# Two stretches of unused bytes in SBUF that move the operands of the expert and the dense matmuls

## The chip, the core and the metric

The kernel runs on one core of a Trainium2 chip. The metric is the device time of one execution in microseconds, as the median of several runs. Three runs of the kernel before gave 948.05 us (947.99 to 948.15).

## The reference

Attention with a threshold, a routed expert layer that picks one of eight experts for each token, and a dense layer, one behind the other, for 4 x 576 = 2304 tokens of 512 features:

```python
def _attn_ref(q, k, v, tau):          # 4 batches, 8 heads, 576 rows, 64 features
    scores = scale * np.matmul(q, k.transpose(0, 1, 3, 2))
    thresh = np.max(scores, axis=-1, keepdims=True) - tau
    scores = np.where(scores >= thresh, scores, -1000000000.0)
    attn = softmax(scores)
    return np.matmul(attn, v)

def _moe_ref(x, modality_id, w_gate, modality_bias, w1, w2):
    logits = x @ w_gate + modality_bias[modality_id]
    e_idx = np.argmax(logits, axis=1)  # gate_w: the softmax value of the chosen expert
    for e in range(8):
        mask = e_idx == e
        h = np.maximum(x[mask] @ w1[e], 0.0)              # 512 -> 1024
        out[mask] = gate_w[mask, None] * (h @ w2[e])      # 1024 -> 512

def _moe2_ref(x, w_in, w_out):
    h = x @ w_in                                          # 512 -> 2048
    g = h * (1.0 / (1.0 + np.exp(-1.702 * h)))
    return g @ w_out                                      # 2048 -> 512
```

(`softmax(scores)` stands for the reference's lines that subtract the maximum, take the exponential and divide by the sum.)

## The kernel before

The kernel has three stages. The order of the work on each engine is written out by hand, and tiles come from pools that a stack of contexts lays out in SBUF one behind the other.

*Attention* (up to some 310 us) works pair by pair of heads; the change leaves its tiles where they are.

*Experts* (some 310 to 536 us). Tokens are gathered by expert into five slots: four of 512 rows and one of 264. A slot has eight steps f, and each step two groups of 12 matmuls. `Ffn.s1` (L974) multiplies the 128 columns f of the first weights, as the operand that is loaded into the array, with the slot's tokens x, as the operand that is streamed past them: each operand is split into a high and a low part in fp32r (`xh` and `xl`, `ah` and `al`), and the 12 matmuls are four pieces of 128 features times the three products high-high, high-low and low-high. ScalarE and VectorE turn the result into `hh` and `hl`. `Ffn.s2_cols` (L1018) takes the second weights `bh` and `bl` as the loaded operand and `hh` and `hl` as the streamed one, again 12 matmuls, two steps later (`LAG = 2`). The weights come from DRAM into `ra` and `rb` (L1228, L1234) and are split by L1241 and L1242.

*Dense* (some 526 to 935 us). Two blocks of 512 tokens, then two of 512 and one of 256, each with 16 steps f. L974 works as before, with `wi_h` and `wi_l` as the loaded operand and x as the streamed one. `Ffn.s2` (L999) is the other way round: `hh` and `hl` are loaded, 128 tokens at a time, and `wo_h` and `wo_l` are streamed, with 512 columns: four tiles of tokens times three products, 12 matmuls (six in the block of 256). While the first block runs, `convert` splits the last of these weights out of `cv_raw` through `cv_a` into high and low parts (L1143 to L1147, L1152, L1153).

The pools that the change concerns are opened in `moe_kernel` at L1188 to L1193: x, h, sg and ids, then `e_raw` (`ra`, `rb`), `e_w` (`ah` to `bl`) and `e_y` of the experts, then `r_work_b`, the small tiles of the router's second pass. Above them, from the other end of SBUF, lie the resident weights and the tiles of `convert`. When the experts are done, the dense weights that had no room (`wi2`, `wo2`) take the place of the `e_` pools. In the trace they carry the names of `wi_h`, `wi_l`, `wo_h` and `wo_l` like the resident ones.

The built program says where each tile starts in a partition. The remainders of these addresses by 256 bytes:

| tiles | kernel before | changed kernel |
|---|---|---|
| `xh`, `xl` | 64 | 224 |
| `hh`, `hl`, `sg` | 64 | 224 |
| `ra`, `rb`, `ah`, `al`, `bh`, `bl`, `y` | 0 | 224 |
| resident dense weights `wi`, `wo`, and `cv_raw`, `cv_a`, `cv_e` | 224 | 224 |
| later dense weights `wi2`, `wo2` | 224 | 224 |
| `ident`; the four `xg` | 128; 64, 128, 192, 0 | the same |

Inside these tiles a matmul's operands start at multiples of 256 bytes from the tile's start (128 columns of 4 bytes are 512 bytes), so that the table holds for each of them.

Of the kernel before, what the change touches and what calls it, by code (L numbers as in the profile page):

```python
# [8 lines left out]
F32 = mybir.dt.float32  # L9
# [514 lines left out]
PG = 512  # L524
NA = 2
NB = 12
SLOT_ROWS = (512, 512, 512, 512, 264)
SLOT_TILES = tuple(-(-r // 128) for r in SLOT_ROWS)
NB_STATIC = len(SLOT_TILES) - NA
# [3 lines left out]
class Router:  # L533
# [19 lines left out]
    def setup_items(self, tmp_pool):  # L553
# [25 lines left out]
        self.pages = T([128, NE], "pages")  # L579
        self.place = T([128, NB * PG // 128], "place")  # L580
        pl = W([128, NB * PG // 128], "pl", I32)
        flat = midf.rearrange("p b c -> p (b c)")
# [14 lines left out]
        def ids():  # L597
# [4 lines left out]
            nc.gpsimd.tensor_copy(pf, pi)  # L602
            nc.gpsimd.iota(pl, pattern=[[128, NB * PG // 128]], base=1, channel_multiplier=1)
            nc.gpsimd.tensor_copy(self.place, pl)
# [97 lines left out]
    def assign(self, ph, gate):  # L702
        nc, wk = self.nc, self.wk[ph]
        first = ph == "A"
        n = NCOL - 5 if first else NCOL
        ns = NA if first else NB
        nh = ns * PG // 128
        t = {}
        T = lambda shape, name, dt=F32: wk.tile(shape, dt, name=name)
        be = lambda a: a.unsqueeze(1).broadcast_to([128, n, NE])  # L710
        rs, cnt = T([128, n, NE], "rs"), T([128, NE], "cnt")
        f, excl, end, base = (T([128, NE], x) for x in ("f", "excl", "end", "base"))
        ok = T([128, n, NE], "ok")
        plf = T([128, 2, n], "plf")
        OL = T([128, n, 128], "OL", BF16)
        R = T([128, n, 2, nh], "R", BF16)
# [53 lines left out]
        def slots():  # L770
            cmp = T([128, ns, NE], "cmp")
            nc.vector.tensor_tensor(
                cmp, end.unsqueeze(1).broadcast_to([128, ns, NE]),
                self.iota[:, 0:ns].unsqueeze(2).broadcast_to([128, ns, NE]), op=ALU.is_le,
            )
            yield
            t["cmp"] = cmp
            ef = T([128, ns], "ef")
            nc.vector.tensor_reduce(out=ef, in_=cmp, axis=AX.X, op=ALU.add)
            yield  # L780
            ei = self.c.tile([128, ns], I32, name="ei" + ph)
            nc.vector.tensor_scalar(ei, ef, float(NE - 1), None, op0=ALU.min)
            yield
            self.idx["e" + ph] = ei

        sh = T([128, ns], "sh")

        def gaps():

# [9 lines left out]
        def bounds():  # L799

            s0, last = NB_STATIC - 1, SLOT_ROWS[-1]
            total, c = T([128, 1], "total"), T([128, 2], "cc")
            nc.vector.tensor_reduce(out=total, in_=cnt, axis=AX.X, op=ALU.add)
            yield
            nc.vector.tensor_sub(c, self.place[:, 4 * s0:4 * s0 + 8:4], sh[:, s0:s0 + 2])
            yield
            nc.vector.tensor_sub(c, c, self.place[:, 0:1].broadcast_to([128, 2]))
            yield
            nc.vector.tensor_tensor(c, c, total.broadcast_to([128, 2]), op=ALU.min)
            yield  # L810
            over = T([128, 2], "over")
            nc.vector.tensor_sub(over[:, 0:1], c[:, 1:2], c[:, 0:1])
            yield
            nc.vector.tensor_scalar(over[:, 0:1], over[:, 0:1], float(last), None, op0=ALU.is_gt)
            yield
            nc.vector.tensor_scalar(over[:, 1:2], c[:, 1:2], float(REST), None, op0=ALU.is_gt)
            yield
            nc.vector.tensor_tensor(over[:, 0:1], over[:, 0:1], over[:, 1:2], op=ALU.max)
            yield
            nc.vector.tensor_scalar(self.range[:, 0:1], over[:, 0:1], -1.0, float(NB_STATIC), op0=ALU.mult, op1=ALU.add)  # L820
            yield
# [73 lines left out]
        def compact():  # L895
            cp = T([128, nh], "cp")
            nc.vector.tensor_sub(
                cp.rearrange("p (s t) -> p s t", t=4), self.place.rearrange("p (s t) -> p s t", t=4),
                sh.unsqueeze(2).broadcast_to([128, ns, 4]))
            yield  # L900
            nc.vector.scalar_tensor_tensor(out=cp, in0=t["s"], scalar=0.0, in1=cp, op0=ALU.is_ge, op1=ALU.mult)
            yield
            icc = self.c.tile([128, nh], I32, name="iccB")
            nc.vector.tensor_scalar(icc, cp, -1.0, None, op0=ALU.add)
            yield
            c0 = T([128, NB_STATIC], "c0")
            nc.vector.tensor_sub(c0, self.place[:, 0:4 * NB_STATIC:4], sh[:, 0:NB_STATIC])
            yield
            ico = self.c.tile([128, NB_STATIC], I32, name="icoB")
            nc.vector.tensor_scalar(ico, c0, -1.0, None, op0=ALU.add)  # L910
            yield
            self.idx["cB"], self.idx["oB"] = icc, ico

        rest = [] if first else [None]
        return [
            None, ranks, pages, starts, limits, slots, inside, counted, places, digits, *rest, high,
            lambda: (low(0, 5), values(0)), *rest, lambda: (low(5, 10), values(1)), *rest, lambda: low(10, n), gate,
            *[None] * (1 if first else NBW), lambda: sum_up(0, n), lists,
            *([] if first else [None] * 12 + [gaps, compact, None, bounds]),
        ]  # L920

# [117 lines left out]
def moe_kernel(ctx, tc, kq, v, tau, mid, w_gate, mod_bias, w1, w2, w_in, w_out, out):  # L1039
    nc = tc.nc  # L1040
    ctx.enter_context(tc.manual_schedule())
    P = lambda name, bufs, c=ctx, **kw: c.enter_context(tc.tile_pool(name=name, bufs=bufs, **kw))
# [142 lines left out]
                self.step()  # L1185


    x_p, h_p, sg_p, id_p = P("x", 2), P("h", 3), P("sg", 1), P("ids", 2)  # L1188
    ffn.hp = h_p
    ectx, fctx = ExitStack(), ExitStack()  # L1190
    EP = lambda name, bufs: P(name, bufs, c=ectx, reuse_waits="tile")
# [78 lines left out]
    def make_slot(s):  # L1270
# [10 lines left out]
        def rest(d, w):  # L1281
# [4 lines left out]

            n = min(128, SLOT_ROWS[s] - d * 128)
            if n > 0:
# [10 lines left out]
            first if s < NA else rest)  # L1299
        return ffn.xprep(blk, x_p, rows[s], wide=(s == 0), count=SLOT_ROWS[s])  # L1300

# [150 lines left out]
    lo = nc.values_load(router.range[0:1, 0:1], min_val=NB_STATIC - 1, max_val=NB_STATIC)  # L1452
    hi = nc.values_load(router.range[0:1, 1:2], min_val=NB_STATIC, max_val=NB)
    with tc.For_i(lo, hi, 1) as i:
# [107 lines left out]
```

## Time and profile before

| | us |
|---|---|
| median of 3 runs | 948.05 |
| the profiled execution | 946.41 |
| its span, first to last instruction | 944.6 |
| TensorE busy in the span | 910.1 |
| weight loads of TensorE busy | 734.9 |
| VectorE busy | 516.2 |
| ScalarE busy | 455.0 |
| GpSimd busy | 224.8 |

The profile tells an operation by its line, its engine, and the tiles that it writes and reads ("tr<-xh,wi_h": the matmul that writes `tr` from `xh` and `wi_h`). Matmuls are pipelined: the profiled duration of one ends after the start of the next, so that durations of neighbours overlap, and the time between two starts is shorter than a duration. PE is TensorE, PEld its loading of weights, DVE VectorE, ACT ScalarE, POOL GpSimd, SP the engine that issues most of the DMAs. A query can narrow the trace to a stretch, counted in us from the span's start.

### The profile page before, as it was taken

Reading aid. Unit: us, or ns where it says so; the run is one execution under the profiler, and the core shown is the slowest. Engines: PE = TensorE matmul, PEld = TensorE weight load, DVE = VectorE, ACT = ScalarE, POOL = GpSimd, SP = SyncE. Lnnn points to the kernel's source line nnn. Section 1 sums busy time; section 2 is a strip of 40 time slices with the busy share of each in tenths; the row PEclk is TensorE's granted clock in tenths of the full one; section 3 lists DMA queues with packets and bytes.
Section 4 is the critical chain, followed back from the end, with each engine's and each line's share of the span. In section 5 each row is a group of like instructions: output and inputs, shape, how many; then the busy total and the mean of one; then the engine's idle time right before and its main releaser. Section 6 shows DMA issues by size and latency. Waiting matters only on the chain.

```text
span 944.6 us, 13971 instructions
## 1 busy us (share of the span) xinstructions
PE 910.1 (96%) x5015; PEld 734.9 (78%) x5015; DVE 516.2 (55%) x1129; ACT 455.0 (48%) x820; POOL 224.8 (24%) x299
## 2 busy tenths in 40 slices
PE   8899999999987999999999999999999999999995
PEld 7777777777765678878889888888888888888894
DVE  6888888888797375578787587611111111111111
ACT  6777777777766443455545455422222222222231
POOL 4946475566414302010520000010001000100100
PEclk9999999999999999999999999999999999999998
DMA  7655864654504444565746254210001000100100
GB/s 229 152 143 145 227 174 116 165 150 121 133 13 114 141 136 135 180 229 174 237 171 230 71 179 132 91 45 12 23 12 45 6 12 6 45 0 1 45 1 25
DMA packets 64523, 100.72 MB, mean 107 GB/s; under 512 B 10596, under 2 KB 35970, under 8 KB 64450
## 3 DMA queue, kind: packets, MB, share of 16 engines
q1 hardware_dynamic: 61138, 89.84, 32.6%
q0 software_dynamic: 3312, 9.94, 3.3%
q8 instruction: 42, 0.69, 0.3%
q14 instruction: 31, 0.25, 0.1%
HBM read 63.97 MB, written 17.11 MB: 86 GB/s over the span
## 4 chain that ended last, share of the span: by engine, by line
PE 77%; DVE 9%; issue 6%; ACT 3%; DMA 2%; POOL 1%; SPq 1%; POOLq 0%; ACTq 0%; DVEq 0%
PE tr L974 27%; PE sc L999 19%; PE sc L239 9%; PE sc L1018 8%; PE av L353 5%; PE tr L307 5%; DVE e L250 3%; DVE E L280 2%; PE tr L383 1%; PE av L349 1%; ACT e L256 1%; PE tr L328 1%; DVE bl L1242 1%; DMA cv_raw<-in_moe_w_in_dram 1%; PE av L946 1%
## 5 line engine op out<-in xcount | busy, mean ns | idle before, releaser
L1209 DVE TENSOR_TENSOR hl<-sg,hh 128x512 fp32r<-128x512 f32 (+1 forms) x80 | 51.1, 639 | 271.2 <-ACT hh L1207 271.2
L1206 ACT ACTIVATE sg<-tr 128x512 f32<-128x512 f32 (+1 forms) x80 | 44.5, 556 | 238.9 <-PE tr L974 238.8
L250 DVE TENSOR_SCALAR_CACHE_REDUCE e<-sc,taue 128x576 f32<-128x576 f32 x144 | 116.6, 813 | 30.2 <-PE sc L239 25.5
L256 ACT ACTIVATE e<-e,thr 128x576 f32<-128x576 f32 x144 | 111.3, 776 | 27.1 <-DVE e L250 26.5
L239 PE MATMUL sc<-kA,qT 128*128 128x288 f32 x320 | 102.1, 336 | 14.9 <-DVE E L280 11.0
L999 PE MATMUL sc<-wo_h,hh 128*128 128x512 f32 x288 | 114.1, 396 | 0.0
L999 PE MATMUL sc<-wo_h,hl 128*128 128x512 f32 x288 | 113.9, 396 | 0.0
L999 PE MATMUL sc<-wo_l,hh 128*128 128x512 f32 x288 | 113.8, 395 | 0.0
L280 DVE SCALAR_TENSOR_TENSOR E<-sc,thr,e 128x576 f32<-128x576 f32 x128 | 103.7, 815 | 8.4 <-ACT e L256 4.6
L309 ACT COPY AT<-tr 128x512 f32<-128x512 f32 x128 | 74.0, 578 | 39.4 <-PE tr L307 38.6
L239 PE MATMUL sc<-kB,qT 128*128 128x288 f32 x320 | 89.4, 295 | 0.9 <-DVE kB L220 0.9
L239 PEld LDWEIGHTS sc<-kA,qT 128*128 128x128 f32 x320 | 60.2, 188 | 31.7 <-issue 19.4
L974 PE MATMUL tr<-xh,wi_h 128*128 128x512 f32 (+1 forms) x320 | 80.8, 375 | 0.0
L974 PE MATMUL tr<-xl,wi_h 128*128 128x512 f32 (+1 forms) x320 | 80.3, 372 | 0.0
L974 PE MATMUL tr<-xh,wi_l 128*128 128x512 f32 (+1 forms) x320 | 80.1, 372 | 0.0
L307 PE MATMUL tr<-ident,E 128*128 128x128 f32 x512 | 76.7, 272 | 0.0
L353 PE MATMUL av<-AT,V 128*64 128x288 f32 x512 | 76.7, 419 | 0.0
L974 PEld LDWEIGHTS tr<-xh,wi_h 128*128 128x128 f32 x320 | 57.8, 188 | 13.0
L974 PEld LDWEIGHTS tr<-xl,wi_h 128*128 128x128 f32 x320 | 56.9, 188 | 11.9
L974 PEld LDWEIGHTS tr<-xh,wi_l 128*128 128x128 f32 x320 | 56.8, 188 | 11.6
L999 PEld LDWEIGHTS sc<-wo_h,hl 128*128 128x128 f32 x288 | 54.2, 188 | 13.2
L999 PEld LDWEIGHTS sc<-wo_l,hh 128*128 128x128 f32 x288 | 54.3, 188 | 12.3
(219 smaller groups left out, 1569.3 us busy)
## 6 DMA issues: line engine op xcount, KB each, us to landing
ra<-in_moe_w_dram SPq DMA_DIRECT2D x20, 512.0 KB
rb<-in_moe_w_dram SPq DMA_DIRECT2D x20, 512.0 KB
F<-in_kq_dram SPq DMA_DIRECT2D x15, 640.0 KB
cv_raw<-in_moe_w_in_dram SPq DMA_DIRECT2D x16, 512.0 KB
cv_raw<-in_moe_w_out_dram SPq DMA_DIRECT2D x16, 512.0 KB
V<-in_vp_dram SPq DMA_DIRECT2D x16, 320.0 KB
kA<-kA SPq DMA_DIRECT2D x15, 320.0 KB
kB<-kB SPq DMA_DIRECT2D x15, 320.0 KB
```

The lines of the kernel that those rows point to most:

```text
L239: nc.tensor.matmul(sc[:, hf, 0:288], l, d[kk][:, c0 + hf * 288:c0 + (hf + 1) * 288], start=(i == 0), stop=(i == len(ops) - 1),)
L250: nc.vector.tensor_scalar(e, d["sc", w][:, :, 0:288], self.taue[:, 0:1], 3.0e38, op0=ALU.add, op1=ALU.min, accum_out=thr)
L256: self.nc.scalar.activation(d["e", w], d["e", w], ACTF.Exp, bias=d["thr", w][:, 0:1], scale=-1.0)
L280: nc.vector.scalar_tensor_tensor(out=E.rearrange("p (a c) -> p a c", a=2), in0=d["sc", w][:, :, 0:288], scalar=d["thr", w][:, 0:1], in1=d[ ...
L307: nc.tensor.transpose(tp[:, kc * 128:(kc + 1) * 128], E[:, k0 + kc * 128:k0 + (kc + 1) * 128], self.ident)
L309: copies.append(lambda: nc.scalar.copy(AT[:, h, :, c * 128:(c + 1) * 128], tp.rearrange("p (k c) -> p k c", k=4)))
L353: nc.tensor.matmul(d["av"][h * 64:(h + 1) * 64, 0:288], d["V"][:, h, kc, :], d["AT"][:, h, kc, hf * 288:(hf + 1) * 288], start=False, stop ...
L974: nc.tensor.matmul(hps[:, 0:T], w[:, kd, :], blk[x][:, kd, 0:T], start=(i == 0), stop=(i == 11))
L999: nc.tensor.matmul(y, h[:, cs], w, start=(f == 0 and i == 0), stop=(f == blk["nf"] - 1 and i == 2))
L1018: nc.tensor.matmul(blk["y"][d], w[:, ds], h[:, 0:T], start=(f == 0 and i == 0), stop=(f == last and i == 2))
L1206: nc.scalar.activation(sg, hps, ACTF.Gelu_apprx_sigmoid)
L1209: return [upper, lambda: nc.vector.tensor_sub(hl, sg, hh.bitcast(F32))]
```

## The change

A pool with one unused tile of 160 bytes is opened ahead of x, and one with an unused tile of 64 bytes behind ids. To make room for them, the router's second pass shares some of its small tiles: `ef` becomes `sh`, and `c0` and `cc` become one tile `three`. The start of the region above, 147424, stays where it is; the small tiles now end at that address.

```diff
+PHASE = (160, 64)
...
+        sh = T([128, ns], "sh")
+        three = T([128, NB_STATIC], "three")
...
-            ef = T([128, ns], "ef")
+            ef = sh
...
-        sh = T([128, ns], "sh")
-
...
-            total, c = T([128, 1], "total"), T([128, 2], "cc")
+            total, c = T([128, 1], "total"), three[:, 0:2]
...
-            c0 = T([128, NB_STATIC], "c0")
+            c0 = three
...
+    P("phase_x", 1).tile([128, PHASE[0] // 4], F32, name="phase_x")
     x_p, h_p, sg_p, id_p = P("x", 2), P("h", 3), P("sg", 1), P("ids", 2)
+    P("phase_w", 1).tile([128, PHASE[1] // 4], F32, name="phase_w")
```

Built, both programs have the same instructions in the same order on every engine. Their semaphores differ in one place: in `bounds` the first subtraction (L805) now waits for the sum ahead of it (L803), both on VectorE.

## Rows read from the trace of the kernel before

**Rows 1.** Page, part 1: busy us, share of the span, instructions.

```profile
PE 910.1 (96%) x5015; PEld 734.9 (78%) x5015; DVE 516.2 (55%) x1129; ACT 455.0 (48%) x820; POOL 224.8 (24%) x299
```

**Rows 2.** Page, part 4: chain that ended last, shares by engine.

```profile
PE 77%; DVE 9%; issue 6%; ACT 3%; DMA 2%; POOL 1%; SPq 1%; POOLq 0%; ACTq 0%; DVEq 0%
```

**Rows 3.** Stretches: length; PE, PEld, DVE, ACT, POOL busy (instructions); PEclk, DMA share, GB/s.

```profile
410.00:450.00 40.00, 40.00 (x184) 32.91 (x183) 31.82 (x56) 22.98 (x35) 3.57 (x4) 1.00 0.67 226
600.00:650.00 50.00, 50.00 (x216) 40.22 (x215) 13.72 (x22) 14.68 (x26) 3.94 (x4) 1.00 0.15 50
```

**Rows 4.** Waits of the whole span: us in total, times, longest us.

```profile
ACT sg L1206 <- PE tr L974: 238.8, 71, 4.4
```

**Rows 5.** The chain in order of time: start us, us, what.

```profile
411.05 2.75 PE sc L1018 x12
413.80 2.75 PE tr L974 x12
...
511.25 1.45 PE tr L974 x12
...
545.47 2.81 PE tr L974 x12
...
876.28 2.80 PE tr L974 x12
```

**Rows 6.** Groups by form, 300 to 944 us: busy us, mean ns | idle before.

```profile
L999 PE MATMUL sc<-wo_h,hh 128*128 128x512 f32 x288 | 114.1, 396 | 0.0
...
L999 PE MATMUL sc<-wo_l,hh 128*128 128x512 f32 x288 | 113.8, 395 | 0.0
L974 PE MATMUL tr<-xh,wi_h 128*128 128x512 f32 x256 | 70.4, 397 | 0.0
L974 PE MATMUL tr<-xl,wi_h 128*128 128x512 f32 x256 | 70.2, 396 | 0.0
L974 PE MATMUL tr<-xh,wi_l 128*128 128x512 f32 x256 | 69.9, 394 | 0.0
```

**Rows 7.** Two seam matmuls by line: ns min/median/max, first and last start us.

```profile
L974 PE MATMUL tr<-xh,wi_l x1: 392/392/392, 536.7 to 536.7; 128*128 128x512 f32 x1
...
L999 PE MATMUL sc<-wo_h,hl x1: 394/394/394, 926.9 to 926.9; 128*128 128x512 f32 x1
```

**Rows 8.** By line, L974 (600 to 870 us), L1018 (410 to 495 us); columns alike.

```profile
L974 PE MATMUL tr<-xh,wi_h x192: 392/396/403, 601.4 to 865.6; 128*128 128x512 f32 x192
...
L1018 PE MATMUL sc<-hh,bh x60: 388/392/394, 410.9 to 491.3; 128*128 128x512 f32 x60
```

**Rows 9.** Last block: order of time (start us, us), then L974 by line.

```profile
895.85 0.66 PE L974 MATMUL tr<-xh,wi_h 128*128 128x256 f32 x4
...
897.29 0.40 PE L999 MATMUL sc<-wo_h,hh 128*128 128x512 f32 x1
...
L974 PE MATMUL tr<-xh,wi_l x64: 278/282/286, 882.7 to 928.4; 128*128 128x256 f32 x64
```

**Rows 10.** By line, L1018 ahead of a transpose, the first and the last.

```profile
L1018 PE MATMUL sc<-hh,bl x1: 393/393/393, 342.0 to 342.0; 128*128 128x512 f32 x1
...
L1018 PE MATMUL sc<-hh,bl x1: 394/394/394, 493.2 to 493.2; 128*128 128x512 f32 x1
```

**Rows 11.** Groups by form, ScalarE and VectorE, 545 to 944 us.

```profile
L1207 ACT CAST hh<-sg 128x512 fp32r<-128x512 f32 x60 | 37.3, 621 | 1.9
...
L1152 ACT CAST wo_h<-cv_a 128x512 fp32r<-128x512 f32 x10 | 6.2, 620 | 19.0 <-DVE cv_a L1147 19.0
...
L1209 DVE TENSOR_TENSOR hl<-sg,hh 128x512 fp32r<-128x512 f32 x61 | 42.2, 692 | 227.5 <-ACT hh L1207 227.5
...
L1153 DVE TENSOR_TENSOR wo_l<-cv_a,wo_h 128x512 fp32r<-128x512 f32 x10 | 6.9, 692 | 6.5 <-ACT wo_h L1152 6.4
```

**Rows 12.** Stretches with a load of ra, then of cv_raw; columns as in rows 3.

```profile
378.80:382.00 3.20, 3.20 (x16) 2.62 (x15) 0.23 (x1) 0.86 (x2) 0.00 (x0) 1.00 0.97 355
559.20:562.00 2.80, 2.80 (x14) 2.25 (x13) 2.65 (x6) 1.95 (x4) 0.00 (x0) 1.00 0.91 322
```

## The prediction

> **What bounds the kernel now.** I read the page's first line: TensorE is busy for 910.1 of 944.6 us [rows 1]. Then the shares of the chain of work that ended last: 77% of the span lies on TensorE [rows 2]. Then stretches of the dense stage: from 600 to 850 us each of five times 50 us has TensorE busy for all 50.00 us, 216 matmuls, at the full granted clock (1.00 of 2.4 GHz), while VectorE and ScalarE are busy for 8 to 15 us; the first of the five stands there [rows 3]. It is the others that wait: ScalarE for L974, 238.8 us in all [rows 4]. So from some 537 us on, time is the number of matmuls times the **pitch**, the time from the start of one to the start of the next, and only a change of pitch moves the end.
>
> The pitch is not one number. In the chain a group of 12 matmuls of 512 columns takes 2.80 or 2.81 us in the dense stage and 2.75 us in the expert stage [rows 5], where TensorE is as full, 40.00 of 40 us [rows 3]. From 545.47 to 876.28 us lie 59 rounds of 24 matmuls: 330.81 / 1416 = 233.6 ns. In the expert stage it is 2.75 / 12 = 229.2 ns. Clock and columns are the same. What differs is where the operands lie. While matmul k streams its moving operand, the weights of matmul k+1 are loaded beside it, so the moving operand of k and the weights of k+1 are the pair that can get in each other's way. By the table of remainders this pair is 64 and 0 in the expert stage, 64 and 224 for L974 in the dense stage, 224 and 64 for L999. I call a step **equal** if both remainders are the same. The dense stage has such steps already, at its seams: from the last L974 of a group to the first L999 (64 and 64), and from the last L999 to the first L974 (224 and 224).
>
> The trace tells the seams from the rest by the profiled durations. A duration runs on past the next start by a nearly fixed time: dense 395.9 against 233.6 ns of pitch, expert 392 against 229.2, so 162 to 163 ns in both. Differences of duration are therefore differences of pitch. The 62 seams from L974 to L999 last 390 to 393 ns, the 77 from L999 to L974 392 to 394 ns; the first of the one kind and the last of the other stand in [rows 7]. Inside the groups the durations spread, for L974 from 392 to 403 ns [rows 8].
>
> **The change part by part.** The 160 bytes ahead of the x tiles take x, h and sg from 64 to 224; with the 64 bytes behind the ids the expert weights go from 0 to 224; the dense weights stay at 224. All steps inside the tiles are multiples of 256 bytes, so every L974, L999 and L1018 step becomes equal. No instruction is added, removed or moved on any engine, and the DMA issues stay in their order.
>
> *Dense, 512 columns.* L974 has 768 of these, 256 each with means of 397, 396 and 394 ns; L999 has 864, of which two thirds show 396 and one third 395 [rows 6]. Take the seams out, 64 at 391.5 ns (62 of them before L999) and 77 at 393: the other 704 of L974 last (768 x 395.7 - 64 x 391.5) / 704 = 396.0, the other 786 of L999 395.9. I use 395.9 for both. What will an equal step cost when it follows an equal step? No long chain of them is in the trace. From below it is bounded by the shortest durations of the expert stage, 388 ns [rows 8]; from above by an equal step of another kind, L1018 followed by a transpose whose f32 weights also lie at 64: there are 16 of these, the first at 393, the last at 394 ns [rows 10], with a mean of 394.3 and a spread of 390 to 399. I take the mean of the two kinds of seams, 392.2: they have the lines, types and widths of the steps in question, and they came out within 4 ns of each other although the steps ahead of them did not. Gain: 1490 x (395.9 - 392.2) = 5.5 us.
>
> *Dense, 256 columns.* 192 of L974 in the last block, 12 of them in 897.29 - 895.85 = 1.44 us [rows 9]. The seam among the 12 lasts 278 ns, the shortest that this pair of tiles shows there [rows 9], so its pitch is 278 - 163 = 115; the other 11 take (1440 - 115) / 11 = 120.5. Gain: 176 x 5.5 = 1.0 us.
>
> *Expert, 512 columns.* 768 matmuls at a median of 392 ns [rows 8]. They give up the good pair of 64 and 0: by pitch 392.2 - 162.4 = 229.8 against 229.2, so 0.6 x 768 = 0.5 us is lost, between nothing and 0.9 us.
>
> *Expert, 264 columns.* 192 of them, 12 in 1.45 us [rows 5], a pitch of 120.8. The seam's 115 at 256 columns would be 118.6 at 264 ones, 0.4 us gained; no equal step of this width is in the trace, so between nothing and 0.4, and I take 0.2.
>
> *VectorE and ScalarE at the new places.* The same operations stand in the trace at 64 and at 224: ScalarE's copies 621 (L1207) and 620 ns (L1152), VectorE's subtractions 692 (L1209) and 692 ns (L1153) [rows 11]. I cost them at nothing; most of each stretch is free for them [rows 3]. The router's shared small tiles put one more wait between two VectorE operations that follow each other anyway, in the stretch from 410 to 450 us, where TensorE is busy without a break [rows 3]: nothing.
>
> *The weight loads.* The expert weights now land at 224 instead of 0. A stretch with a load of ra at 0 moved 355 GB/s at a busy share of 0.97, one with a load of cv_raw, which is at 224 already, 322 at 0.91 [rows 12]: 366 and 354 for a full share. The 3% between them on 1.5 us for 512 KB is 0.05 us for each of 40 loads, issued groups ahead of their use: costed at nothing, 2 us if all of it were uncovered. The Trainium skill (DMA: Bandwidth & Descriptors, How a descriptor splits into AXI transactions) says that a descriptor which does not start at a multiple of 256 bytes pays for a first transaction from the boundary below; by that, a piece of 1 KB at 224 costs 39 beats in place of 32, and 20 loads of ra, uncovered, some 6 us, an estimate from that page that would eat the gain. The trace's 354 against 366 shows a far smaller difference.
>
> **Sum.** 5.5 + 1.0 - 0.5 + 0.2 = 6.2 us. Nothing is late in its place: what feeds TensorE in the dense stage waits for it [rows 4]. The profiled execution took 946.41 us, 1.8 of it outside the span, and would take 940.2; the median of the runs, 948.05, becomes 941.9.
>
> **Rivals.** *Deeper:* a chain of equal steps settles at the 388 ns that the expert stage shows in part of its steps. Dense 7.9 x 1490 = 11.8, expert 4 x 768 = 3.1, the narrow ones 1.2: 16.1 us, 932.0. For it: a pair of operands can reach 388. Against: none of the 139 seams did.
>
> *Shallower:* the chain takes the mean of [rows 10], 394.3. Dense 1.6 x 1490 = 2.4, 256 columns 0.4, expert -2.3 x 768 = -1.8: 1.0 us, 947.0. For it: that is an equal step too, and its spread shows that equality alone does not fix a duration. Against: its weights are f32 and belong to a transpose.
>
> *Nothing:* the remainders don't set the pitch; the seams are short because a group ends there, and the expert groups because of their order of operands. Time 948.0. The Trainium skill (TensorE: Matmul & The Clock Gate, Step-by-step: what each phase is for) has this as a rule: loading the next weights takes no read bandwidth from the running matmul, each having a port of its own. Against it stands that the expert stage has seams too, from L974 to L1018 and back, with 64 and 0 like the rest, and L1018 and L974 groups take the same 2.75 us [rows 5]; groups of this stage that are built like dense ones (L974) are faster throughout, not at their ends.
>
> *Slower:* equal remainders keep the two reads in step, and a long chain of them, which no row shows, locks in on a long duration, as 4 of the 16 of [rows 10] have it (397 to 399). At 398: dense 2.1 x 1490 = 3.1 lost, expert 6 x 768 = 4.6, together 7.7 us, 955.8. It decides from 394.6 ns upward, where 1490 x (395.9 - c) no longer pays for 768 x (c - 392). Against: 139 seams, none above 394.
>
> **How the numbers follow.** Forecast 0.71, with 939 to 945 as its own range; deeper 0.06; shallower 0.10; nothing 0.06; slower 0.07. About 0.2% (1.9 us) is what a measurement of this kernel can tell from no change. Faster by more: forecast and deeper, 0.77. Within: shallower and nothing, 0.16. Slower: 0.07. The range from 937.0 to 947.5 takes in the shallower case and leaves out deeper, nothing and slower, 0.19 together.
>
> **What would show it.** In the profile after: groups of 12 in the chain at 2.76 us in the dense stage, at 2.75 to 2.77 in the expert stage; some 219 matmuls in 50 us instead of 216; L974 and L999 at 512 columns with means of 391 to 393 and hardly a spread; L974 at 256 columns near 278; the stretch from 537 us to the end shorter by some 6 us and everything ahead of the expert stage unchanged. I am wrong if the dense means stay at 396 (nothing), if the expert groups grow by more than the dense ones shrink (slower), or if TensorE waits for ra or rb (the loads).

## The result and the profile after

The changed kernel takes 936.72 us as the median of five runs (935.7 to 940.83), the kernel before 948.05 in the same comparison: a ratio of 0.9882, with a 95% interval of 0.986 to 0.9903. It is 11.3 us faster. The forecast was 6.2 us, to 941.9, with a range from 937.0 to 947.5: the direction was right, the gain is almost twice the forecast, and the time lies 0.3 us below the range.

The profiled execution was the longest of the five, 940.83 us. In its first 50 us the granted clock was 0.97 of 2.4 GHz on average and TensorE got 287 matmuls done in place of 308; the changed tiles are not in use there. The stretches of both kernels (columns as in [rows 3]), before first:

```profile
0.00:50.00 50.00, 42.99 (x308) 36.53 (x310) 38.20 (x97) 34.02 (x60) 34.00 (x50) 1.00 0.68 181
...
334.01:534.28 200.27, 200.07 (x1005) 167.25 (x1006) 140.26 (x234) 98.47 (x153) 28.72 (x34) 1.00 0.53 175
534.28:881.87 347.59, 347.59 (x1490) 279.68 (x1490) 101.18 (x168) 106.05 (x181) 11.73 (x12) 1.00 0.14 44
881.87:944.60 62.73, 51.03 (x312) 45.27 (x311) 8.88 (x19) 14.47 (x35) 5.85 (x6) 0.94 0.07 27
```

And the same of after:

```profile
0.00:50.00 50.00, 42.04 (x287) 35.80 (x288) 35.30 (x89) 31.06 (x52) 31.97 (x49) 0.97 0.69 181
...
339.92:539.29 199.37, 199.00 (x1005) 167.07 (x1006) 139.96 (x234) 98.32 (x153) 29.91 (x34) 1.00 0.54 176
539.29:876.57 337.28, 337.28 (x1490) 279.28 (x1490) 101.03 (x168) 105.66 (x181) 11.72 (x12) 1.00 0.14 46
876.57:939.10 62.53, 50.55 (x312) 45.15 (x311) 8.87 (x19) 14.40 (x35) 5.84 (x6) 0.93 0.07 27
...
600.00:650.00 50.00, 50.00 (x223) 41.39 (x222) 15.97 (x26) 15.49 (x26) 3.94 (x4) 1.00 0.17 54
```

The last three stretches of each begin and end at the same matmuls (x1005, x1490, x312 in both): from the first group of 12 of the expert stage to the last dense L974 group ahead of the first L999 (L1000 after), on to the block of 256 tokens, and to the end. They are shorter by 0.90, 10.31 and 0.20 us, 11.41 in all. The profiled execution had come to the first of them 5.91 us later (339.92 against 334.01), so that its span is only 944.6 - 939.1 = 5.50 us shorter. Some 3.3 us of these had come up by the 308th matmul, the rest are mostly longer waits of TensorE in the attention stage. e1 below, which has these edits of the router too, has neither, so they are not put down to the change. The medians, which one slow start does not set, differ by 11.3 us, close to the 11.41 us, and nine tenths of these lie in the dense stage. From 600 to 650 us TensorE now runs 223 matmuls, where it ran 216 [rows 3].

The chain of after in order of time (start us, us, what), which answers to [rows 5]:

```profile
348.22 0.44 PE av L947 x4
348.65 2.77 PE tr L975 x12
351.42 2.72 PE sc L1019 x12
...
550.17 2.72 PE tr L975 x12
...
871.13 2.72 PE tr L975 x12
...
876.57 1.43 PE tr L975 x12
878.00 2.75 PE sc L1000 x12
```

Between 550.17 and 871.13 lie 59 rounds of 24 matmuls, as between 545.47 and 876.28 before: 320.96 / 1416 = 226.7 ns of pitch against 233.6. The first group behind four transposes (L947) takes 2.77 us, the next one 2.72.

The groups by form after (busy us, mean ns | idle before), which answer to [rows 6]:

```profile
L1000 PE MATMUL sc<-wo_h,hh 128*128 128x512 f32 x288 | 112.2, 390 | 0.0
L1000 PE MATMUL sc<-wo_l,hh 128*128 128x512 f32 x288 | 112.2, 390 | 0.0
...
L975 PE MATMUL tr<-xh,wi_h 128*128 128x512 f32 x256 | 68.4, 389 | 0.0
```

By line (ns min/median/max, first and last start us), dense from 600 to 870 us and expert from 410 to 495 us, which answer to [rows 8]:

```profile
L975 PE MATMUL tr<-xh,wi_h x197: 389/389/389, 599.6 to 866.2; 128*128 128x512 f32 x197
...
L1019 PE MATMUL sc<-hh,bh x60: 389/389/395, 409.9 to 490.6; 128*128 128x512 f32 x60
```

The spread of L974, 392 to 403 ns [rows 8], is gone: 197 dense matmuls last 389 ns each. That is less than the seams of before (391.5 and 393 on average).

### The profile page after: what moved, and what is told of

Read it like the earlier page. It is cut to its first block, busy times and chain, and to the rows that moved or that the text cites. A ratio compares the mean times of both kernels' runs of the same rounds, so it can differ in the third digit from the quotient of the medians.

```text
span 939.1 us, 13971 instructions
## 1 busy us (share of the span) xinstructions
PE 900.9 (96%) x5015; PEld 735.8 (78%) x5015; DVE 515.6 (55%) x1129; ACT 454.2 (48%) x820; POOL 224.7 (24%) x299
## 4 chain that ended last, share of the span: by engine, by line
PE 77%; DVE 8%; issue 6%; DMA 3%; POOL 2%; ACT 2%; SPq 1%; POOLq 0%; ACTq 0%; DVEq 0%
PE tr L975 28%; PE sc L1000 19%; PE sc L1019 9%; PE sc L239 8%; PE av L353 5%; PE tr L307 4%; DVE e L250 3%; DVE E L280 2%; PE tr L383 1%; PE av L349 1%; ACT e L256 1%; PE tr L328 1%; DMA xg<-x_dram,igaA 1%; PE av L947 1%; SPq L176 1%
## 5 line engine op out<-in xcount | busy, mean ns | idle before, releaser
L1000 PE MATMUL sc<-wo_h,hh 128*128 128x512 f32 x288 | 112.2, 390 | 0.0
L1000 PE MATMUL sc<-wo_l,hh 128*128 128x512 f32 x288 | 112.2, 390 | 0.0
L1000 PE MATMUL sc<-wo_h,hl 128*128 128x512 f32 x288 | 112.0, 389 | 0.0
L975 PE MATMUL tr<-xh,wi_h 128*128 128x512 f32 (+1 forms) x320 | 78.6, 368 | 0.0
L239 PEld LDWEIGHTS sc<-kB,qT 128*128 128x128 f32 x320 | 61.0, 191 | 3.0 <-DVE kB L220 1.3
L1000 PEld LDWEIGHTS sc<-wo_h,hl 128*128 128x128 f32 x288 | 54.1, 188 | 11.4
```

Source lines behind the costliest of these rows:

```text
L239: nc.tensor.matmul(sc[:, hf, 0:288], l, d[kk][:, c0 + hf * 288:c0 + (hf + 1) * 288], start=(i == 0), stop=(i == len(ops) - 1),)
L975: nc.tensor.matmul(hps[:, 0:T], w[:, kd, :], blk[x][:, kd, 0:T], start=(i == 0), stop=(i == 11))
L1000: nc.tensor.matmul(y, h[:, cs], w, start=(f == 0 and i == 0), stop=(f == blk["nf"] - 1 and i == 2))
```

## The experiments

"First groups" are those of L974 and what became of it, "second groups" those of L999 (dense) and L1018 (expert). Differences are the remainder of the streamed operand less that of the loaded one, by 256; for the expert stage they stand behind the time. To make room, e1 to e5 let two more small tiles of the router share one place and open the second stretch of unused bytes with the expert pools. e1 to e5 and e9 to e12 are medians of 4 to 10 runs, e6 to e8 one run each beside 948.23 of the kernel before. Times in us:

| run | dense: first, second groups | 12 dense: first, second | 12 expert, undisturbed | median | ratio (95%) |
|---|---|---|---|---|---|
| before | 96, 160 apart | 2.80, 2.80 | 2.75 at 64 | 948.05 | |
| after | equal | 2.72, 2.72 | 2.72 at 0 | 936.72 | 0.9882 (0.986 to 0.9903) |
| e1 | equal | 2.72, 2.72 | 2.75 at 64 | 936.96 | 0.9881 (0.9865 to 0.9898) |
| e2 | as before | 2.80, 2.80 | 2.72 at 0 | 947.56 | 0.9991 (0.9981 to 1.0) |
| e3 | equal by 256, not by 512 | 2.72, 2.72 | 2.72 at 0 | 938.05 | 0.988 (0.9862 to 0.9898) |
| e4 | 224, 32 apart | 2.80, 2.80 | 2.79 at 128 | 949.7 | 1.0011 (1.0 to 1.0021) |
| e5 | 64, 192 apart | 2.78, 2.80 | 2.81 at 160 | 949.63 | 1.0014 (1.0 to 1.0028) |
| e6 | 16, 240 apart | 2.78, 2.79 | 2.78 at 16 | 948.96 | |
| e7 | 4, 252 apart | 2.84, 2.80 | 2.84 at 4 | 956.34 | |
| e8 | 48, 208 apart | 2.79, 2.80 | 2.76 or 2.80 at 48 | 948.63 | |
| e9 | equal, tiles of e6 to e8 | 2.72, 2.72 | 2.72 at 0 | 936.81 | 0.9879 (0.9863 to 0.9896) |
| e10 | hl alone 64 off | 2.73, 2.77 | | 942.31 | 0.9938 (0.9921 to 0.9954) |
| e11 | hl and wo_l 64 off | 2.73, 2.76 | | 940.95 | 0.9927 (0.9911 to 0.9944) |
| e12 | equal in each group, two remainders | 2.73, 2.76 | | 942.14 | 0.9939 (0.9923 to 0.9956) |

### Each half of the change alone

```diff
-PHASE = (160, 64)
+PHASE = (160, 0)
```

in e1, the dense part (x, h at 224, expert weights at 160), and in e2, the expert part (x, h and expert weights at 64):

```diff
-PHASE = (160, 64)
+PHASE = (0, 64)
```

> x and h at 224 as in the changed kernel, the expert weights at 160 (difference of 64 between the streamed operand and the next weights, as in the kernel before). Theory (the difference of the two remainders sets the pitch; a chain of equal steps settles at 226.7 ns): dense groups of 12 at 2.72 us, expert groups of 512 columns at 2.75 us as before the change, the time 768 x 2.3 ns = 1.8 us above the changed kernel, some 938.5 us. Rival (the remainder 224 of the streamed operand itself is the good one): dense and expert groups both at 2.72 us, some 936.7 us.

> x and h stay at 64 as in the kernel before, the expert weights go from 0 to 64. Theory (the difference sets the pitch, whatever the remainder): expert groups at 2.72 us though nothing lies at 224 there, dense groups at 2.80 us as before; some 946.1 us. Rival (224 itself is good): expert groups at 2.75 us as before, dense 2.80 us, some 948 us.

The chain of e1, an expert and a dense pair of groups (L976 first groups, L1020 and L1001 second ones):

```profile
422.74 2.75 PE sc L1020 x12
425.49 2.75 PE tr L976 x12
...
548.31 2.72 PE sc L1001 x12
551.03 2.72 PE tr L976 x12
```

And of e2, two of each stage:

```profile
423.37 2.72 PE sc L1020 x12
426.09 2.72 PE tr L976 x12
...
431.53 0.44 PE av L948 x4
431.97 2.75 PE tr L976 x12
...
608.28 2.80 PE tr L976 x12
611.08 2.79 PE sc L1001 x12
```

The dense part carries the gain: e1 is as fast as the whole change. In e2 the expert groups go at 2.72 us although no operand of theirs lies at 224 (x and the expert weights lie at 64), so it is the difference of the remainders that counts. Both times missed what the theory wanted: e1 was due 1.8 us above the changed kernel and came 0.2 above, and e2, 948.03 - 947.56 = 0.5 us below the kernel before, was due 1.9 below. By the times alone the rival (224 itself is good) would fit better; the groups refute it. The 0.5 us is no more than the noise, as the interval of e2 reaches 1.0. Two things make the expert part so small. Half of the first groups stand behind four transposes and mostly take 2.75 to 2.77 us there, no less than before. And the expert stage of e2 (columns as in [rows 3]), though TensorE is busy in it for 199.20 us against the 200.07 of before, is no shorter:

```profile
334.94:535.39 200.45, 199.20 (x1006) 167.14 (x1006) 140.28 (x234) 98.17 (x153) 29.68 (x34) 1.00 0.53 175
```

TensorE idles there for 1.25 us in place of 0.20, nearly all of it in waits for VectorE's `xl` and `y`.

### Which period

```diff
-XW = DM + 16
-PHASE = (160, 64)
+XW = DM + 4
+PHASE = (256, 64)
```

By 512, x, h and the expert weights of e3 lie at 224, the dense weights at 480.

> x, h and the expert weights at 224 by 512, the dense weights at 480 by 512: in the dense stage equal by 256, but apart by 256 bytes. To make room, the gathered rows are 516 instead of 528 columns wide. Theory (256 is the period): dense groups at 2.72 us, expert groups at 2.72 us, some 936 to 937 us. Rival (the period is 512 or more): dense groups at 2.75 us or above, expert groups at 2.72 us, 940 us or above.

Groups of 2.72 us in both stages: a remainder by 256 is what has to be equal; one by 512 may differ. Equality by 128 does not do: the expert stage of e4 (below), 128 apart, takes 2.79 us. The median, 938.05, is 1 us above what was expected. The profiled execution of e3 began with a granted clock of 0.97 too; from the start of the expert stage to the end of the span it takes as long as after, 599.1 us against 599.0.

### Other differences

```diff
-PHASE = (160, 64)
+PHASE = (128, 192)
```

in e4 (x, h at 192, expert weights at 64), and in e5 (x, h at 32, expert weights at 128):

```diff
-PHASE = (160, 64)
+PHASE = (224, 160)
```

> x and h at 192, expert weights at 64. Difference of streamed operand less next weights: -32 in dense L975, +32 in dense L1000, 128 in the expert stage. Theory in its strict form (only 0 locks in): dense groups at 2.76 us or above, expert groups at 2.74 us or above, 942 to 950 us. Rival (near is as good as equal): dense groups at 2.72 us.

> x and h at 32, expert weights at 128. Differences (streamed operand less next weights, by 256): 64 in dense L975, which the expert stage had before; 160 in the expert stage, which dense L999 had before; 192 in dense L1000, in no run so far. Theory (the difference sets the pitch, not the stage or the line): dense L975 groups at 2.75 us, expert groups at 2.80 us. Rival (each stage has its own pitch): L975 at 2.80 us, expert groups at 2.75 us. Open for both: L1000. Total between 942 and 952 us.

The last matmul of a dense first group of e4, by line; it streams from 192, and the weights loaded beside it lie at 192 too:

```profile
L976 PE MATMUL tr<-xh,wi_l x1: 397/397/397, 608.9 to 608.9; 128*128 128x512 f32 x1
```

By the prediction's pair this step is equal, and it lasts 397 ns, no less than the others of its group (395 to 397). All 62 such steps of e4 last 397 ns. So equality of that pair is no reason for a short step by itself. In e5 the stages swap differences. The expert groups take 2.81 us at 160, as dense ones do at that difference. The dense first groups at 64 take 2.76 and 2.79 us in turn, not the 2.75 of the expert stage of before: no difference other than zero was seen to have one fixed price.

Finer steps, with x, hh and hl moved inside tiles that are 256 bytes longer:

```diff
-        hh = self.hp.tile([128, 512], F32R, name="hh")
+        hh = self.hp.tile([128, 576], F32R, name="hh", tag="hh")[:, FINE:FINE + 512]
...
-        R["cv"], R["raw"] = RP("cv", 3), RP("cv_raw", 2)
+        R["cv"], R["raw"] = RP("cv", 2), RP("cv_raw", 2)
```

`FINE` is 4 elements in e6, 1 in e7, 12 in e8 and 0 in e9; `hl` and the x tiles go likewise.

> All operands as in the changed kernel, but x and h 16 bytes further: difference 16 in L975 and in the expert stage, -16 (240) in L1000. To make room the tiles of convert have two buffers in place of three. If a chain locks in over a range of differences: 2.72 us per group of 12. If only equal remainders lock in: 2.75 us or above. Total 936 to 950 us.

> As the run with 16 bytes, but 4 bytes apart (one element): difference 4 in L975 and in the expert stage, -4 (252) in L1000. If the lock needs the same element: 2.75 us per group or above. If it needs the same line of some 16 to 64 bytes: 2.72 us. Total 936 to 950 us.

> As the run with 16 bytes, but 48 bytes apart: difference 48 in L975 and in the expert stage, -48 (208) in L1000. Between 32 (233.2 ns in L1000 of the run with 192 and 64) and 64 (229 ns in the expert stage before) the pitch should lie between those two: 2.75 to 2.80 us per group. Total 940 to 950 us. Against it: a pitch below 2.72 us, which would be a better place than equal.

> The tiles of e6 to e8 (x, hh and hl 256 bytes longer, two cv_a tiles in place of three), but with an offset of 0: all operands at one remainder again, as in the changed kernel. If the offset alone made e6 to e8 slow: groups of 12 of 2.72 us, means of 389 to 390 ns, 935 to 938 us. If it was the longer tiles or the missing third cv_a: 945 us or more with groups of 2.78 us or more, or waits of TensorE from 537 us on.

The chain of e7 (L981 first groups, L1006 second ones), where one element lies between the remainders:

```profile
606.56 2.80 PE sc L1006 x12
609.36 2.84 PE tr L981 x12
```

The expert stage of e8, 48 apart, has groups of two lengths (L981 first, L1025 second groups):

```profile
415.78 2.76 PE tr L981 x12
...
435.56 2.80 PE sc L1025 x12
```

And the chain of e9, the same program as e7 with an offset of 0:

```profile
600.75 2.72 PE tr L981 x12
603.47 2.72 PE sc L1006 x12
```

e9 settles that the longer tiles and the missing `cv_a` cost nothing, so that the 19.5 us between e7 and e9 come from one element of offset (the kernel before took 948.23 and 948.03 us beside them). e7 lies 6 us above its expected 936 to 950. Nearness to zero is worth nothing: a difference of 4 bytes is the slowest of all, and 252, one element the other way, takes the 2.80 us of 160. Every difference tried that is not zero takes 2.76 to 2.84 us in the dense stage.

### How much of the chain has to be equal, and which pair counts

In the dense second groups the loaded operands are hh, hh, hl, and the streamed ones wo_h, wo_l, wo_h, four times over. Moving some of them by 64 bytes makes some steps unequal:

```diff
+HLF = 16
...
-        hl = self.hp.tile([128, 576], F32R, name="hl", tag="hl")[:, FINE:FINE + 512]
+        hl = self.hp.tile([128, 576], F32R, name="hl", tag="hl")[:, HLF:HLF + 512]
```

That is e10 (against e9). e11 moves wo_l as well, e12 hh and wo_h too, the dense weights so:

```diff
+def low_rows(pool, n, name):
+    t = pool.tile([128, n * 512 + 64], F32R, name=name)
+    return t[:, HLF:HLF + n * 512].rearrange("p (f c) -> p f c", f=n)
...
-        R["wo"] = [res.tile([128, NWO, 512], F32R, name=n) for n in ("wo_h", "wo_l")]
+        R["wo"] = [res.tile([128, NWO, 512], F32R, name="wo_h"), low_rows(res, NWO, "wo_l")]
```

> Only hl starts 64 bytes on; all other operands keep one remainder. In a dense second group the loaded operands are hh, hh, hl, four times over, so that one step in three is unequal; in the first groups none is. If each step has its own price: two thirds of the second groups' steps stay at 226.7 ns, a group of 12 takes some 2.75 us, the first groups stay at 2.72 us, and the dense gain shrinks by some 2 us, to 938 to 940 us. If only an unbroken chain goes at 226.7 ns: the second groups take 2.79 to 2.80 us, the first ones do not settle in their 12 steps (2.74 us or more), 943 to 947 us. Which pair it is: by the pair of the running matmul and the next one's weights the long durations are those of sc<-wo_l,hh, whose successor loads hl; by the matmul's own pair they are those of sc<-wo_h,hl.

> As e10, but wo_l too starts 64 bytes on. In the dense second groups every streamed operand then has the remainder of the weights that are loaded next, while two of three matmuls have another remainder than the weights that they themselves use. If the pair is that of the running matmul and the next one's weights, as the prediction took it: no dense step is unequal, groups of 2.72 us, all means 389 to 390 ns, 936 to 939 us. If it is the matmul's own pair: both sc<-wo_l,hh and sc<-wo_h,hl are unequal, the second groups take 2.78 us or more, more than the 2.77 of e10, 943 to 947 us.

> x and the first weights keep 224; hh, hl and all second dense weights start 64 bytes on. Every dense matmul then has one remainder for both of its own operands, while at both seams of each round of 24 the running matmul and the next weights differ. If it is the matmul's own pair: 2.72 us for all dense groups, the seam matmuls 389 ns. If it is the pair with the next weights: two breaks in 24 steps, each followed by some three steps that do not run at 226.7 (as in the first groups of e10, 2.73 us), groups of 2.73 to 2.76 us. In the expert stage the second groups stand 64 apart and go at 229 ns in both cases, so that the time is 937 to 938.5 by the first and 938.5 to 942 us by the second.

e10, groups by form of the dense stage, and under it the chain (L982 first, L1007 second groups):

```profile
L1007 PE MATMUL sc<-wo_h,hl 128*128 128x512 f32 x236 | 93.8, 397 | 0.0
L1007 PE MATMUL sc<-wo_l,hh 128*128 128x512 f32 x236 | 92.3, 391 | 0.0
L1007 PE MATMUL sc<-wo_h,hh 128*128 128x512 f32 x236 | 91.8, 389 | 0.0
...
L982 PE MATMUL tr<-xh,wi_h 128*128 128x512 f32 x236 | 63.8, 392 | 0.0
```

```profile
603.52 2.73 PE tr L982 x12
606.25 2.77 PE sc L1007 x12
```

The long step is the one that uses hl (397 ns), not the one beside which hl is loaded (391). And the first groups, which hold no unequal operand, take 2.73 us in place of 2.72: their first steps (xh, wi_h: a mean of 392 ns) pay for what stood ahead of them. One odd operand in every third step of the second groups gives back more than a third of the dense gain: a round of 24 takes 5.50 us, against 5.44 (all equal) and 5.60 (before). The expert stage, where hl is streamed, gives back its part too (2.77 us for a second group). The median, 942.31, lies between the bands of the two theories: neither "each step has its own price" (938 to 940) nor "all or nothing" (943 to 947).

e11, the same views (L987 first, L1012 second groups):

```profile
L1012 PE MATMUL sc<-wo_h,hh 128*128 128x512 f32 x238 | 93.7, 394 | 0.0
L1012 PE MATMUL sc<-wo_l,hh 128*128 128x512 f32 x238 | 93.3, 392 | 0.0
L1012 PE MATMUL sc<-wo_h,hl 128*128 128x512 f32 x238 | 93.0, 391 | 0.0
```

```profile
604.75 2.76 PE sc L1012 x12
607.51 2.73 PE tr L987 x12
```

Here every streamed operand has the remainder of the weights that are loaded next, so by the prediction's pair no dense step is unequal, and 2.72 us were due. The second groups take 2.76, and the longest matmuls (394) are those whose own operands are equal. The rival, the matmul's own pair, does no better: it wanted 2.78 us or more, with wo_l,hh and wo_h,hl the long ones. The median, 940.95, lies between the two bands as well (936 to 939 and 943 to 947).

e12, one second group by line, its first, third, fifth, seventh and last step:

```profile
L1012 PE MATMUL sc<-wo_h,hh x1: 389/389/389, 605.7 to 605.7; 128*128 128x512 f32 x1
...
L1012 PE MATMUL sc<-wo_h,hl x1: 397/397/397, 606.2 to 606.2; 128*128 128x512 f32 x1
...
L1012 PE MATMUL sc<-wo_l,hh x1: 387/387/387, 606.6 to 606.6; 128*128 128x512 f32 x1
...
L1012 PE MATMUL sc<-wo_h,hh x1: 398/398/398, 607.1 to 607.1; 128*128 128x512 f32 x1
...
L1012 PE MATMUL sc<-wo_h,hl x1: 389/389/389, 608.3 to 608.3; 128*128 128x512 f32 x1
```

All these operands lie at 32, every step but the last is equal by both pairs, and still they last 387 to 398 ns, until the last two stand at 389. What stood ahead of the group were operands at 224. The time, 942.14, is 0.1 above the upper end of the band for the next pair, and the groups (2.73, 2.76) fit it, but in e11 that pair was equal at every step and 2.72 us did not come; the own pair (2.72 in all) falls here. What fits e10 to e12 and the groups behind transposes is a memory: after a change of the operands' remainders the steps need a while, the first three of a first group in e10 and some ten here, to come to 389 ns again. What carries it was not tried.

## Why the prediction came out too small

*What bounds the kernel.* Right. TensorE has no gap in the stretch from 539.29 to 876.57 us (337.28 of 337.28 busy, as before), and the end moved with the pitch.

*That equal remainders shorten the pitch.* Right, and shown by e1, e2 and e9 against e7: with the same matmuls in the same order, the place of the operands alone moves the pitch from 226.7 to 233.6 ns. Where the loaded operand lies counts by itself: with the streamed ones at 224 in both, expert groups take 2.75 us with the weights at 160 (e1) and 2.72 with the weights at 224 (after). The Trainium skill (TensorE: Matmul & The Clock Gate, Step-by-step: what each phase is for) has it that loading the next weights takes no read bandwidth from the running matmul. These runs do not agree, as far as the load of some weights slows the stream; that it is the load of the next ones is not shown. Another rival, that the other engines get in TensorE's way, is not borne out: from 534 to 882 us of before, the steps during most of which VectorE, ScalarE or GpSimd is busy have a mean pitch of 233.5 ns, the others 233.3.

*The step that failed* is "What will an equal step cost when it follows an equal step?", answered with "the mean of the two kinds of seams, 392.2". A long chain of equal steps settles at 389 ns, a pitch of 226.7. The term "Dense, 512 columns", forecast at 5.5 us, came to about 10.3 (the middle stretch, which holds nine tenths of these matmuls). The rival *deeper* (388 ns, 11.8 us for this term) had the size of this term nearly right, though its whole, 932.0, is 4.7 us too low. The prediction's own bound from below, 388 ns, held; its range, which ended at 937.0, left that bound out. *Deeper* got a chance of 0.06 because "none of the 139 seams" reached 388; but a seam is a single equal step between unequal ones, and e10 and e12 show that a step also carries what stood ahead of it. The seams were no sample of the chain. Nor does the equality of their pair alone make them short: the equal seams of e4 last 397 ns.

*The pair.* That a step is short when "the moving operand of k and the weights of k+1" are equal is refuted by e4 and e11. Whether these two reads are the ones that meet stays open: in e11 the remainders change from step to step, and in e12 a change alone upsets steps that are equal by both pairs. The pair did no harm to the sign, since the change makes all operands of the two stages equal, and so every pair that one can name; that was luck, as far as the pair goes.

*Dense, 256 columns.* Forecast 1.0 us, measured about 0.2: groups of 1.43 against 1.44 us, 119.4 ns between two starts against 120.5. The one short seam of 278 ns was again taken for the price of a chain. After the change all matmuls of this kind last the same, and no less than before [rows 9]:

```profile
L975 PE MATMUL tr<-xh,wi_l x64: 283/283/283, 877.4 to 922.7; 128*128 128x256 f32 x64
```

Equal is not even the best place at this width: 64 apart (e5) it is 117.9 ns between two starts, 16 apart (e6) 117.6, in one execution each.

*Expert, 512 columns.* Forecast a loss of 0.5 us, since the 64 and 0 of before looked as good as an equal pair. The sign was wrong: undisturbed groups go from 2.75 to 2.72 us, those behind transposes stay, and TensorE is busy for about 1 us less in the stretch (199.00 after, 199.20 in e2, 200.07 before). How much of it is left is a matter of the waits, and so of luck: the stretch is 0.90 us shorter in the profiled execution of after, and 0.18 longer in that of e2. *Expert, 264 columns:* forecast 0.2; the groups still take 1.44 to 1.45 us (120.8 ns between two starts against 121.2). A chain of equal steps brings 1 ns or less at these narrower widths.

*VectorE and ScalarE at the new places.* Right. Groups of after that answer to [rows 11]:

```profile
L1210 ACT CAST hh<-sg 128x512 fp32r<-128x512 f32 x62 | 38.5, 621 | 2.0
```

```profile
L1212 DVE TENSOR_TENSOR hl<-sg,hh 128x512 fp32r<-128x512 f32 x62 | 42.8, 691 | 219.0 <-ACT hh L1210 219.0
```

*The weight loads.* Right at nothing to 0.2 us: TensorE idles for 199.37 - 199.00 = 0.37 us of the expert stage, against 0.20 before, and the DMAs moved 176 GB/s at a busy share of 0.54, against 175 at 0.53. The 6 us that the prediction worked out from the Trainium skill (DMA: Bandwidth & Descriptors, How a descriptor splits into AXI transactions) for loads at 224, were they uncovered, do not show. The Trainium skill tells there of bytes that are fetched, and the change moves only the place where they land.

*The other rivals.* Shallower (394.3 ns) and nothing fall with the means of 389 and 390. The slower one, a chain that locks in on a long duration, does not occur at a difference of zero; at 4 bytes (e7) something like it does, 2.84 us in each first group. The sum with the measured terms is 10.3 for the dense stage up to the last block, 0.9 for the expert stage (in this execution) and 0.2 for the end, 11.4 us against the measured 11.3. The 10.3 is firm: the middle stretch takes 337.28 us in e1 and e9 as well.

None of the twelve kernels beats the changed one: e1 and e9 are as fast, within 0.3 us.

## What to carry to other kernels

Where TensorE is full and a long row of 512-column matmuls in fp32r swaps weights at every step, lay out all of its operands, streamed and loaded, at one remainder by 256 bytes, and do it for the whole row: part of the operands gives part of the gain, and a difference of 4 bytes is worse than one of 96 (2.84 against 2.80 us for 12). A few odd steps inside a different pattern do not tell what a long unbroken row will cost, since a step depends on what ran ahead of it; where such a row is not in the trace, keep its range as wide as the shortest duration seen at that width. The price of a change in layout is read from the time between starts (or, as here at 512 columns, from durations that follow it), not from the busy share, which is 100% of the dense stretch in both kernels.

## What the hardware showed that was not expected

- Unbroken, equal chains of 512 columns go at 226.7 ns, each matmul at the same 389 ns; no other difference of the table goes as fast. At 256 columns equality brings 1.1 ns of 120.5, and two unequal layouts (e5, e6) do better; at 264 columns 0.4 of 121.2.
- One element (4 bytes) between the remainders makes a first group 2.84 us, against 2.72 at zero and 2.78 at 16 bytes: 956.34 us for the kernel, in the one run that there is.
- The pitch has a memory. Behind four transposes a group of equal steps takes 2.77 us, the next one 2.72; behind a change from operands at 224 to operands at 32 it takes some ten steps until they last 389 ns (e12), behind the change back three.
- What stays open: which two reads meet. Neither the streamed operand with the weights that are loaded next (e11) nor the one with its own weights (e10 to e12) explains the durations step by step, and why one kind of change is over after three steps and another after ten was not tried.
